# Low halves of expert 0 on GpSimd and a later start for expert 2's load, in a convolution and mixture-of-experts kernel

## The chip, the cores and the metric

One core of a Trainium2 chip runs the whole program. The metric is the device time of one execution in microseconds, the median of several runs. The engines are named as in the profile: PE (TensorE matrix products), PEld (its weight loads), DVE (VectorE), ACT (ScalarE), POOL (GpSimd), SP (SyncE, which here only issues DMAs). A q behind a name (SPq, ACTq) is that engine's sequencer.

## The reference

```python
# attention: softmaxed 7-tap causal filters, one for each of 8 heads of 24 channels
w = softmax(weight)                                  # 8 x 7
x_pad = concat([zeros(B, 6, 192), x], axis=1)        # x: 8 x 2880 x 192
attn[b, s, h, :] = sum_k w[h, k] * x_pad[b, s + k, h, :]
# mixture of experts over N = 23040 tokens of 192 values
g = argmax(attn @ w_group)          # 4 groups
e = argmax(attn @ w_expert[g])      # 4 experts in a group
y = relu(attn @ w1[g, e]) @ w2[g, e]     # 192 -> 1024 -> 192
out = softmax_g[g] * softmax_e[e] * y
```

All tensors are float32. Each token goes to one of 16 experts.

## The kernel before

**Units.** The tokens are cut into blocks of 120 (BT) and the blocks into units of 4, 8 or 12 (SIZES; unit 5 has 8 blocks, units 6, 7, 8, 9 and 10 have 12 each). `unit(u)` is a generator, and `step()` (L1147) moves the live units on by turns. A unit reads its input (`load_unit`, L254, DMAs at L250 and L252 on SP's queue; the tile xin has two buffers, and unit u asks for the input of unit u + 1 in its first step), convolves it with band matrices on PE (L506), copies the result from PSUM on ACT into xc or a spare tile and xcb (L511, L513), and stores both in DRAM in xcd (L515, L678, issued on ACT's queue). xc has two buffers (`room_tile`, L184), taken by every second unit, so that units 2, 4 and 6 follow each other there. Transposes (L527, L538) and small products (L600, L606) give the logits; DVE makes from them the choice and the weight of each token (L645 to L674, the last being the reciprocal that L678 stores with the rows) and its place in an expert's list (L685 to L736). POOL scatters the list into a table in DRAM with an indirect DMA (L738).

**Slots.** When five units are through, the list of the first portion is read back (L1209), and the main loop (L1402) begins: a slot is 256 tokens of one expert. Slot i gathers its rows by an indirect DMA from POOL (`gather`, L818, L829), transposes them on PE (`turn`, L848 and L850) and runs `hidden` (L872) and `back` (L892) in four steps f2 each. In the first portion there is one slot for each of experts 0 to 7, then more portions follow, and the units not yet routed are worked between the slots' steps. `finish` (L948) weighs the result and scatters it to the output (L965).

**High and low halves.** Products keep float32 precision by splitting each operand into a rounded high half and the rest, the low half. For an expert's weights, `weights()` (L757) takes four raw tiles out of a pool of six buffers, loads w1 into the first two (128 and 64 rows of 1024 values) and w2 into the last two (L765, L766, L771, all through `load`, L749, on SP's queue), and leaves four `split(k)` to be done: ah and al (k = 0), bb (k = 1) and the two halves of cw (k = 2, 3). Each has a copy on ACT (L786, L790, L798) and then a subtraction (L787, L791, L799), whose engine is `eng.get(k, nc.vector)`: DVE unless the dictionary `eng` names another. The first half of `hidden` likewise is an ACT rectifier (L886) and a DVE operation for its low half hl (L887); the list `lows` holds the latter in order.

**What sets the order.** Expert 0's weights are asked for in step 60 of the routing and split in steps 100 to 130, expert 1's are asked for in step 140 (KPRE, L1304 to L1314) and split in the 96 further steps before the main loop (L1319 to L1324). `{k: nc.gpsimd for k in PREG[e]}` (L1311) is their `eng`. Expert 0's raw tiles take buffers 2 to 5 of the pool, expert 1's 0 to 3 and expert 2's 4, 5, 0 and 1. Expert 2's weights are asked for in `open_slot(2)`, called in the first step of slot 0 (L1448), by L1296:

```python
weights(..., held=pi == 0 and e > 1, after=(gathers[0] if e == 2 else lows[2] if e == 3 else None) if pi == 0 else None)
```

`after` puts a wait on the loads for the named instruction: `gathers[0]` is the last gather of slot 0, `lows[0]` the first low half hl of slot 0. `held` keeps the loads of w2 back until the last step of slot i (L1456), where those of expert 2 wait for `lows[0]` too. The program's text gives each instruction a place, but the order on each engine's queue is chosen by the compiler's planner, which takes what is ready first by its own costs; `pin`, `issue_after` and `keep_in_program_order` are the exceptions written into the code. An engine works its queue in that order.

Of the kernel before, what the change touches and what calls it, by code (L numbers as in the profile page):

```python
# [35 lines left out]
def conv_moe_kernel(  # L36
# [20 lines left out]
    def pin(on, ins):  # L57

        return tc.keep_in_program_order(ins) if on and pinned[0] else ins

    B, S, D = x.shape
# [4 lines left out]
    F = w1.shape[3]  # L66
# [42 lines left out]
    PENG = lambda pi, e: None  # L109
# [16 lines left out]
    GL = 6  # L126
    GB = 4
    MARGIN = 5
    PREG = ((), ())
    RB = False  # L130
    PRE2 = 0
    NSK = 2
# [612 lines left out]
    lows = []  # L745

    gathers = []

    def load(dst, src, after=None):  # L749
        ins = nc.sync.dma_start(out=dst, in_=src)  # L750
        if after is not None:
            tc.add_manual_dep(
                ins.ins, after.ins.name,
                mybir.DependencyInfo(mybir.DependencyClass.Sync, mybir.DependencyReason.DATA), reason="later load")
        return ins

    def weights(r1, r2, eng=None, held=False, after=None):  # L757
        eng = eng or {}
        raw = [wraw.tile([P, F], F32, name="raw") for _ in range(4)]
        ra, rb = raw[0], raw[1]  # L760
        HF = NF // 2
        rc = [r[:, 0:HF * D].rearrange("p (f d) -> p f d", d=D) for r in raw[2:]]
        npin[0] += 1
        hold = tc.keep_in_program_order if NPIN[0] < npin[0] <= NPIN[1] else lambda ins: ins
        hold(load(ra, w1f[bass.ds(r1, P), :], after))  # L765
        hold(load(rb[0:D2], w1f[bass.ds(r1 + P, D2), :], after))  # L766

        def fetch(after=after):
            for k in range(2):
                loads.append(load(  # L770
                    rc[k], w2f[bass.ds(r2 + k * HF * P, HF * P), :].rearrange("(f p) d -> p f d", p=P), after))  # L771

        W = {}
        if held:
            W["fetch"] = fetch
        else:
            fetch()

        def split(k):
            if k == 0:  # L780
                W["ah"] = ah = wsp.tile([P, F], F32R, name="ah")
                W["al"] = al = wsp.tile([P, F], F32R, name="al")
                if 8 in eng:
                    nc.gpsimd.tensor_copy(out=ah, in_=ra)
                else:
                    pin(PINA, nc.scalar.activation(out=ah, in_=ra, func=AF.Copy))  # L786
                eng.get(k, nc.vector).tensor_tensor(out=al, in0=ra, in1=ah.bitcast(F32), op=ALU.subtract)  # L787
            elif k == 1:
                W["bb"] = bb = wsp.tile([P, F], F32R, name="bb")
                pin(PINB, nc.scalar.activation(out=bb[0:D2], in_=rb[0:D2], func=AF.Copy))  # L790
                eng.get(k, nc.vector).tensor_tensor(  # L791
                    out=bb[D2:P], in0=rb[0:D2], in1=bb[0:D2].bitcast(F32), op=ALU.subtract)
            else:
                if k == 2:
                    W["cw"] = wsp.tile([P, NF, 2, D], F32R, name="cw")
                cw = W["cw"]
                fs = slice((k - 2) * HF, (k - 1) * HF)
                pin(PINW, nc.scalar.activation(out=cw[:, fs, 0, :], in_=rc[k - 2], func=AF.Copy))  # L798
                eng.get(k, nc.vector).tensor_tensor(  # L799
                    out=cw[:, fs, 1, :], in0=rc[k - 2], in1=cw[:, fs, 0, :].bitcast(F32), op=ALU.subtract,  # L800
                )

        W["todo"] = [lambda k=k: split(k) for k in range(4)]
        return W
# [331 lines left out]
    def stages_to(n):  # L1136
        extra = sum(max(0, stages(n) - i * (SKEW2 + (SKEWX if n >= THIN else 0))) for i in range(1, LIVE2)) if n < NU else 0
        return sum(stages(u) for u in range(n)) + extra
# [8 lines left out]
    def step():  # L1147

        if routed[0] < NU and len(live) < lead[1] and (not live or max(live, key=lambda a: a[0])[1] >= (lead[0] and lead[0] + (SKEWX if routed[0] > THIN else 0) or SK[min(routed[0], len(SK)) - 1])):
            u = routed[0]  # L1150
            live.append([u, 0, unit(u, xin0 if u == 0 else None)])
            routed[0] += 1
        if not live:
            return
        done[0] += 1
        cur = live.pop(0)
        cur[1] += 1
        try:
            next(cur[2])
            live.append(cur)  # L1160
        except StopIteration:
            pass
# [68 lines left out]
    def tail_regs(get, n):  # L1231
        return [
            nc.values_load(
                get(c), engines=[ET.SP], min_val=0, max_val=mv, skip_runtime_bounds_check_because=OOB_WHY,
            )
            for c, mv in ((0, (E - 1) * D), (1, (E - 1) * F), (2, DUMMY))[:n]
        ]
# [28 lines left out]
    opened, gathered, turned = {}, {}, {}  # L1266
# [7 lines left out]
    def open_slot(i):  # L1274
        if i >= len(plan):
            return
        pi, e, s = plan[i]
        if closing:
            wait[0] -= 1
            if wait[0] <= 0 or closing[0] == pi:  # L1280
                open_portion(closing.pop())
        while (len(portions) - 1 if pi == "tail" else pi) not in idps:
            step()
            if closing:
                open_portion(closing.pop())
        rate[0] = max(
            [(stages_to(portions[q][0]) - done[0]) / (max(starts[q] - MARGIN - i, 1) * 2 * NF)
             for q in starts if q not in idps] + [0.0])
        while pi == "tail" and e not in ready:
            next(late[0])  # L1290
        if pi == "tail":
            W = weights(*tail_regs(lambda c: tab[0][0:1, e, c:c + 1], 2)) if s == 0 else opened[i - 1][0]
            ids = [idps["tail"][0:n, e, k:k + 1] for k, n in tail_cols(PIECES[e], s)]
            known = N
        else:
            W = pre.pop(e if pi == 0 else None, None) or weights(e * D, e * F, PENG(pi, e), held=pi == 0 and e > 1, after=(gathers[0] if e == 2 else lows[2] if e == 3 else None) if pi == 0 else None) if s == 0 else opened[i - 1][0]  # L1296
            ids = [idps[pi][:, e - portions[pi][1], k:k + 1] for k in (2 * s, 2 * s + 1)]
            known = sum(n for _, n in units[:portions[pi][0]]) * BT
        opened[i] = (W, ids)
        gathered[i] = gather(ids, known, width(i), i >= E)  # L1300

    pre = {}
    k = 0
    while routed[1] < portions[0][0]:  # L1304
# [3 lines left out]
        for i in [i for i, kk in enumerate(KPRE) if kk == k]:  # L1308
            e, q = divmod(i, 5)
            if q == 0 and e < 2:  # L1310
                pre[e] = weights(e * D, e * F, {k: nc.gpsimd for k in PREG[e]}, held=e > 0)  # L1311
            elif e < 2 and 4 * e + q <= KN:
# [20 lines left out]
    held = None  # L1333
# [68 lines left out]
    for i, (pi, e, s) in enumerate(plan):  # L1402
# [3 lines left out]
        W, ids = opened[i]  # L1406
        w = width(i)
        if i == len(plan) - 1:
            while W["todo"]:
                split_one(W)  # L1410
            held = []
# [80 lines left out]
```

## Time and profile before

| what | value |
|---|---|
| median of 3 runs | 1067.4 us (1065.37 to 1073.29) |
| the profiled execution | 1075.81 us, of which the span from first to last instruction is 1074.1 |
| busy in the span | PE 97%, DVE 69%, ACT 62%, POOL 48% |
| granted TensorE clock | 0.999 of full speed |

Busy times are the time in which an engine had an instruction under way; the ends of PE's instructions are modelled. In the timelines a row has the start, the time from there to the end of the last instruction merged into it, the engine, the line, the operation, the tile written and those read, their sizes and the count; brackets hold the engine's idle time just before and what ended it. A wait for several things is put down to the one that came last by the profile. The DMA share is the mean busy share of the core's 16 DMA engines.

### The profile page before, as it was taken

The page shows a single profiled execution, that of the slowest core. Times are in us where ns is not written, and L with a number is a line of the kernel's source. Part 1 is how long each engine was busy: PE and PEld are TensorE (multiplying, and loading weights), DVE is VectorE, ACT ScalarE, POOL GpSimd, SP SyncE. Part 2 cuts the span into 40 slices and gives each one's busy share as a digit, 9 for nine tenths or more (in the row PEclk, how much of TensorE's full clock was granted, in tenths as well). Part 3 has the DMA queues.
Part 4 walks back from the last instruction along what each step waited for, and adds up shares of the span by engine and source line. Part 5 has one row for each costly group of instructions (what it writes and reads, how often), then busy time and mean ns, then how long its engine had stood idle before and what let it go on. Part 6 is the DMA issues. An engine that isn't in the chain of part 4 may idle for free. (4 is left out here: it accounts for less than half of the span.)

```text
span 1074.1 us, 22328 instructions
## 1 busy us (share of the span) xinstructions
PE 1040.1 (97%) x7908; PEld 1013.9 (94%) x7908; DVE 745.0 (69%) x1790; ACT 661.7 (62%) x1486; POOL 520.2 (48%) x485
## 2 busy tenths in 40 slices
PE   6989999999999999999999999999999999999997
PEld 6878999999999999999999999999999999999997
DVE  4768888979888878867876666656566656556553
ACT  4556577755666656566666666656565666556653
POOL 2114334336546445565556655555565555455432
PEclk9999999999999999999999999999999999999999
DMA  8998897779889578345536432323233332323210
GB/s 200 259 227 215 205 225 203 180 213 235 204 211 203 127 191 187 106 116 106 156 76 176 114 99 75 115 68 110 67 100 104 95 100 71 92 78 98 65 32 26
DMA packets 192755, 148.53 MB, mean 138 GB/s; under 512 B 84616, under 2 KB 178099, under 8 KB 192638
## 3 DMA queue, kind: packets, MB, share of 16 engines
q1 hardware_dynamic: 126608, 92.89, 34.2%
q0 software_dynamic: 19392, 36.09, 12.5%
q10 hardware_dynamic: 46638, 18.07, 7.7%
q8 instruction: 63, 1.03, 0.4%
q14 instruction: 54, 0.44, 0.1%
HBM read 100.47 MB, written 36.46 MB: 127 GB/s over the span
## 5 line engine op out<-in xcount | busy, mean ns | idle before, releaser
L899 PE MATMUL po<-cw,hh 128*128 128x384 f32 x944 | 294.2, 369 | 0.4 <-ACT ys L957 0.4
L881 PE MATMUL ph<-xa,ah 128*128 128x256 f32 x944 | 258.8, 295 | 3.3 <-DVE hl L887 2.1
L886 ACT ACTIVATE hh<-ph 128x512 fp32r<-128x512 f32 x236 | 140.2, 596 | 174.3 <-PE ph L881 133.5
L903 PE MATMUL po<-cw,hl 128*128 128x192 f32 x944 | 236.4, 250 | 0.7 <-issue 0.7
L887 DVE SCALAR_TENSOR_TENSOR hl<-ph,hh 128x512 fp32r<-128x512 f32 x236 | 161.0, 687 | 104.5 <-ACT hh L886 79.0
L829 POOL DMA_INDIRECT xg<-xcd,idpt x137 | 145.1, 1059 | 179.3 <-ACT ys L957 74.8
L829 POOL DMA_INDIRECT xg<-xcd,idp x116 | 132.7, 1144 | 183.7 <-ACT ys L957 97.7
L881 PE MATMUL ph<-xb,bb 128*128 128x256 f32 x944 | 189.6, 282 | 0.5 <-issue 0.4
L881 PEld LDWEIGHTS ph<-xa,ah 128*128 128x128 f32 x944 | 178.4, 189 | 7.1 <-DVE hl L887 2.7
L903 PEld LDWEIGHTS po<-cw,hl 128*128 128x128 f32 x944 | 180.1, 191 | 1.7 <-issue 0.2
L899 PEld LDWEIGHTS po<-cw,hh 128*128 128x128 f32 x944 | 177.6, 188 | 2.3 <-ACT ys L957 0.6
L881 PEld LDWEIGHTS ph<-xb,bb 128*128 128x128 f32 x944 | 146.1, 190 | 1.0 <-issue 0.9
L965 POOL DMA_INDIRECT out<-ys,idpt x99 | 109.8, 1109 | 56.3 <-DVE ys L964 31.6
L881 PE MATMUL ph<-xa,al 128*128 128x256 f32 x472 | 133.9, 284 | 0.5 <-issue 0.5
L965 POOL DMA_INDIRECT out<-ys,idp x88 | 106.3, 1208 | 39.9 <-issue 16.2
L919 PE MATMUL ph<-xa,ah 128*128 128x384 f32 (+1 forms) x368 | 122.2, 335 | 2.9 <-DVE xc L925 1.5
L957 ACT ACTIVATE ys<-po,xg 128x384 f32<-128x384 f32 x164 | 92.0, 581 | 33.2 <-PE po L943 13.5
L864 ACT ACTIVATE xb<-pm 64x128 fp32r<-64x128 f32 (+2 forms) x342 | 94.9, 277 | 6.1 <-DVE xc L674 3.0
L881 PEld LDWEIGHTS ph<-xa,al 128*128 128x128 f32 x472 | 89.3, 189 | 1.7
L919 PE MATMUL ph<-xb,bb 128*128 128x384 f32 (+1 forms) x368 | 90.2, 326 | 0.0
L964 DVE TENSOR_TENSOR ys<-ys 128x192 f32<-128x192 f32 x179 | 61.3, 356 | 28.6 <-ACT ys L957 24.7
L799 DVE TENSOR_TENSOR cw<-raw,cw 128x768 fp32r<-128x768 f32 x80 | 76.1, 953 | 6.4 <-ACT cw L798 5.1
(264 smaller groups left out, 2115.6 us busy)
## 6 DMA issues: line engine op xcount, KB each, us to landing
raw<-in_moe_w SPq DMA_DIRECT2D x80, 384.0 KB
raw<-in_moe_w SPq DMA_DIRECT2D x40, 512.0 KB
raw<-in_moe_w SPq DMA_DIRECT2D x40, 256.0 KB
xcd<-xc ACTq DMA_DIRECT2D x11, 742.5 KB
xin<-in_x SPq DMA_DIRECT2D x7, 1134.0 KB
xin<-in_x SPq DMA_DIRECT2D x6, 1039.5 KB
xcd<-xcb ACTq DMA_DIRECT2D x13, 360.0 KB
xg<-xcd,idpt POOLq DMA_INDIRECT x137
```

The costliest lines, as they stand in the source:

```text
L799: eng.get(k, nc.vector).tensor_tensor(out=cw[:, fs, 1, :], in0=rc[k - 2], in1=cw[:, fs, 0, :].bitcast(F32), op=ALU.subtract,)
L829: ins = nc.gpsimd.indirect_dma_start(out=rows[0:n, to:to + size], out_offset=None, in_=xcd[0:known, :], in_offset=bass.IndirectOffsetOnAxi ...
L864: nc.scalar.activation(out=xb[h:h + D2, 0, c:c + k], in_=pb, func=AF.Copy)
L881: nc.tensor.matmul(out=hp[:, j], lhsT=wgt[:, fs], rhs=xx, start=i == 0, stop=i == len(ops) - 1)
L886: nc.scalar.activation(out=hh, in_=hp, func=AF.Relu)
L887: lows.append(nc.vector.scalar_tensor_tensor(out=hl, in0=hp, scalar=0.0, in1=hh.bitcast(F32), op0=ALU.max, op1=ALU.subtract,))
L899: nc.tensor.matmul(out=oo[t][:, 0:2 * D], lhsT=hh[:, j, ts], rhs=cw[:, f].rearrange("p a d -> p (a d)"), start=f == 0, stop=False,)
L903: nc.tensor.matmul(out=oo[t][:, 0:D], lhsT=hl[:, j, ts], rhs=cw[:, f, 0, :], start=False, stop=f == NF - 1,)
L919: nc.tensor.matmul(out=hp[:, 0:w], lhsT=wgt[:, fs], rhs=xx, start=i == 0, stop=i == len(ops) - 1)
L957: nc.scalar.activation(out=y, in_=oo[t][0:n, 0:2 * D], func=AF.Copy, scale=g)
L964: nc.vector.tensor_tensor(out=y[:, 0:D], in0=y[:, 0:D], in1=y[:, D:2 * D], op=ALU.add)
L965: nc.gpsimd.indirect_dma_start(out=outviews[nscat[0] % len(outviews)], out_offset=bass.IndirectOffsetOnAxis(ap=ids[t].bitcast(U32), axis=0 ...
```

## The change

Two settings are changed. PREG names, for expert 0, all four splits, so that its four subtractions (L787, L791 and L799 twice) are issued on POOL; the copies stay on ACT. And the loads of expert 2's w1 wait for `lows[0]` in place of `gathers[0]`.

```diff
@@ -126,7 +126,7 @@
     GL = 6
     GB = 4
     MARGIN = 5
-    PREG = ((), ())
+    PREG = ((0,1,2,3), ())
     RB = False
     PRE2 = 0
     NSK = 2
@@ -1293,7 +1293,7 @@
             ids = [idps["tail"][0:n, e, k:k + 1] for k, n in tail_cols(PIECES[e], s)]
             known = N
         else:
-            W = pre.pop(e if pi == 0 else None, None) or weights(e * D, e * F, PENG(pi, e), held=pi == 0 and e > 1, after=(gathers[0] if e == 2 else lows[2] if e == 3 else None) if pi == 0 else None) if s == 0 else opened[i - 1][0]
+            W = pre.pop(e if pi == 0 else None, None) or weights(e * D, e * F, PENG(pi, e), held=pi == 0 and e > 1, after=(lows[0] if e == 2 else lows[2] if e == 3 else None) if pi == 0 else None) if s == 0 else opened[i - 1][0]
             ids = [idps[pi][:, e - portions[pi][1], k:k + 1] for k in (2 * s, 2 * s + 1)]
             known = sum(n for _, n in units[:portions[pi][0]]) * BT
         opened[i] = (W, ids)
```

## Rows read from the trace of the kernel before

**Rows 1.** The page, busy us, share of the span, instructions.

```profile
PE 1040.1 (97%) x7908; PEld 1013.9 (94%) x7908; DVE 745.0 (69%) x1790; ACT 661.7 (62%) x1486; POOL 520.2 (48%) x485
```

**Rows 2.** Stages: busy us of each engine, granted clock, DMA share, GB/s.

```profile
40.00:60.00 20.00, 16.03 (x139) 13.89 (x139) 19.24 (x72) 11.53 (x35) 2.65 (x2) 1.00 1.08 266
...
80.00:84.00 4.00, 4.00 (x36) 3.67 (x35) 3.85 (x13) 3.86 (x12) 1.39 (x2) 1.00 0.38 28
84.00:88.00 4.00, 4.00 (x46) 3.99 (x46) 3.73 (x12) 2.83 (x8) 3.29 (x3) 1.00 0.65 137
...
100.00:120.00 20.00, 19.66 (x178) 18.79 (x177) 19.68 (x62) 11.94 (x25) 5.99 (x6) 1.00 1.09 275
```

**Rows 3.** Timeline of PE, 40 to 130 us.

```profile
49.19 0.59 PE L506 MATMUL pm<-xin,band 126*120 126x192 f32 x2 [1.00 <-DVE eold L723]
...
53.15 0.47 PE L732 MATMUL po<-ohv,ohl 120*128 120x32 f16 x12 [1.11 <-DVE ohv L713]
...
58.23 0.63 PE L527 MATMUL pm<-ident,spare 120*128 120x120 f32 x4 [1.61 <-ACT ta L530]
...
87.41 0.31 PE L848 MATMUL pm<-ident,xg 128*128 128x128 f32 x1
...
125.86 0.67 PE L506 MATMUL pm<-xin,band 126*120 126x288 f32 x2
```

**Rows 4.** Timeline of DVE, 40 to 115 us.

```profile
43.10 1.22 DVE L787 TENSOR_TENSOR al<-raw,ah 128x1024 fp32r<-128x1024 f32 x1
...
45.16 1.22 DVE L791 TENSOR_TENSOR bb<-raw,bb 64x1024 fp32r<-64x1024 f32 x1
...
47.12 0.44 DVE L674 RECIPROCAL xc<-se 120x48 f32<-120x48 f32 x1
...
53.00 0.95 DVE L799 TENSOR_TENSOR cw<-raw,cw 128x768 fp32r<-128x768 f32 x1
...
54.89 0.13 DVE L736 SCALAR_TENSOR_TENSOR lsi<-po,none 128x32 int32<-128x32 f32 x1
...
97.19 0.69 DVE L887 SCALAR_TENSOR_TENSOR hl<-ph,hh 128x512 fp32r<-128x512 f32 x1 [0.42 <-ACT hh L886]
...
110.54 1.22 DVE L787 TENSOR_TENSOR al<-raw,ah 128x1024 fp32r<-128x1024 f32 x1
```

**Rows 5.** Timeline of ACT and its queue, 45 to 125 us.

```profile
47.59 0.32 ACTq L678 DMA_DIRECT2D xcd<-xc  x1
...
57.30 0.41 ACT L511 ACTIVATE xc<-ph 120x288 f32<-120x288 f32 x1 [6.16 <-DVE ohx L657]
...
121.02 1.06 ACT L786 ACTIVATE ah<-raw 128x1024 fp32r<-128x1024 f32 x1 [4.78 <-PE pm L606]
```

**Rows 6.** Timeline of POOL, 0 to 85 us.

```profile
1.40 0.28 POOL masks.py:199 TENSOR_SCALAR_AFFINE_SELECT ident<-ident 128x128 f32<-128x128 f32 x1
...
3.57 2.17 POOL L456 MEMSET xg<- 128x588 f32 x4
...
43.47 1.69 POOL L738 DMA_INDIRECT idtab<-lsi,rowi  x1 [9.09 <-DVE lsi L736]
55.30 0.97 POOL L738 DMA_INDIRECT idtab<-lsi,rowi  x1 [10.14 <-DVE dd L646]
...
71.74 0.96 POOL L738 DMA_INDIRECT idtab<-lsi,rowi  x1 [8.16 <-DMA idtab<-lsi,rowi]
...
82.62 1.17 POOL L829 DMA_INDIRECT xg<-xcd,idp  x1 [2.41 <-DMA idp<-idtab]
```

**Rows 7.** Timeline of SP's queue, 84 to 112 us.

```profile
87.55 0.36 SPq L750 DMA_DIRECT2D raw<-in_moe_w  x1
...
88.47 0.45 SPq L252 DMA_DIRECT2D xin<-in_x  x1
...
104.43 7.77 SPq L750 DMA_DIRECT2D raw<-in_moe_w  x3
```

**Rows 8.** Waits of SP's queue, 20 to 140 us: total, times, longest.

```profile
SPq L750 <- DMA xg<-xcd,idp: 16.3, 1, 16.3
```

## The prediction

> **What bounds the kernel now.** I read the page's busy shares first: TensorE (PE) is busy 1040.1 us of 1074.1 [rows 1], so all its idle time together is 34.0 us and no edit of the preparation of weights can win more than the part of it that it touches. The table by stages comes next, because the edits act in the first 125 us. From 40 to 60 us PE is busy 16.03 of 20, VectorE (DVE) 19.24, GpSimd (POOL) 2.65, and the DMA engines are full (share 1.08); from 80 to 88 us their share is 0.38 and then 0.65, and from 100 to 120 it is 1.09 again [rows 2]. Third, PE's timeline with what ended each idle time: 1.00 us at 49.19 and 1.11 us at 53.15 ended by DVE, 1.61 us at 58.23 by ScalarE (ACT) [rows 3]. These are most of the 3.97 us that PE loses there, and I take the rest of the program as paid by PE's own work. So the question is whether DVE's share of these waits shrinks, and whether the loads that the second edit moves make a new one.
>
> **Part one, the low halves of expert 0 on POOL.** DVE loses four subtractions: 1.22 us (al, at 43.10), 1.22 us (bb, at 45.16) and two of 0.95 us (cw, the last at 53.00) [rows 4], in all 4.34 us out of a stretch in which it is 96% busy. POOL gets them: 1024 + 1024 + 768 + 768 = 3584 elements a partition. No row shows a two-input operation of POOL. The memset of xg writes 588 elements four times in 2.17 us, 0.92 ns an element, and gives 3.3 us; the affine select, with one input, takes 0.28 us for 128, 2.2 ns an element, and gives 7.8 us; twice that, if two inputs cost two passes, gives 15.8 us [rows 6]. I take 7.8, since the affine select is the nearest row (it reads and writes), and keep 3.3 and 15.8. What hides it is POOL's idle time: its scatter of unit 1 ends at 43.47 + 1.69 = 45.16 and the one of unit 2 starts after 10.14 idle us at 55.30 [rows 6]. All four behind the first scatter end at 45.2 + 7.8 = 53.0; at 15.8 they end at 61.0 and the scatter of unit 2 is 5.7 us late.
>
> Two chains run through the freed DVE time. The first: the reciprocal at 47.12 gates the store of unit 2's rows, issued at 47.59 on ACT's queue [rows 4, 5]. ACT then idles 6.16 us until 57.30, where it writes an xc tile [rows 5]; the row names a DVE operation, but the pool has two buffers of this tile and the one wanted is the one that the store reads, so I read the wait as the store's landing. PE's 1.61 us end with it. Two of the subtractions (2.44 us) stand ahead of the reciprocal. The second chain: the list of unit 2 at 54.89 gates its scatter at 55.30; each later scatter waits for the landing of the one before (8.16 us before 71.74), then come the list's reload, the gather at 82.62, and the transposes at 87.41, which PE reaches without idling [rows 3, 4, 6]. Both chains thus meet at 87.41, and a gain must come from both. The second has all four subtractions ahead of it, but POOL itself is free only at 53.0, so it moves by 55.3 - 53.0 = 2.3 us. I take the smaller, **-2.3 us**. It is nothing if the landings, in full DMA queues, do not move; -4.3 if all of DVE's saving arrives; and +5.7 us at the dear end of POOL's price.
>
> Other waits on these four: expert 1's w2 goes into the buffers of expert 0's w1 and waits on SP for al and bb, behind it the input of unit 7. With POOL's two at 2.2 us each (1024 elements) behind the first scatter, bb ends at 49.6 instead of 46.4; but that input waits anyway for the convolution at 49.19, which ends at 49.78 [rows 3]. Nothing. The halves' own readers are the first slot's matmuls, past 87.41. Nothing.
>
> **Part two, expert 2's w1 held.** Its two loads (128 and 64 rows of 4 KB: 512 and 256 KB) wait at the head of SP's queue for 16.3 us for the first gather and go at 87.55 [rows 7, 8]. They will wait for the first low half, 97.19 + 0.69 = 97.88 [rows 4], 10.3 us later. The first subtraction that reads them runs on DVE at 110.54 [rows 4]; 768 KB at the 275 GB/s of 100 to 120 us [rows 2] take 2.9 us, so they have some 12 us for 3 and their own use costs nothing. What stands behind the waiting load matters more. Its other instructions behind it are the rest of expert 2's loads, with the same wait, expert 3's with a later one, and inputs of units. On record the input of unit 10 (126 rows by 11 blocks of 768 bytes, 1039.5 KB, beside its small first block) goes behind it, at 88.47 [rows 7]. In the program this load is older, and its buffer is free before the first low half exists, so I expect the planner to put it ahead: out at about 82 us, where the DMA engines idle 0.62 and 0.35 of two 4 us stretches [rows 2], 3.9 us of work; the load needs 3.9 us at 275 GB/s. Its reader runs at 125.86 [rows 3], so it wins nothing by itself, but it now runs beside the first gather (82.62 to 87.41). Bounds: 0, if it fills idle time alone, and 3.9 us, if it goes wholly first. As nearly all of it fits the hole I take a quarter, **+1.0 us**.
>
> Then the backlog. Between 88 and 98 us the engines lose 1.04 MB to the hole before and 0.77 MB to later; the stretch from 98 us on, full until past 120, has 0.77 MB more to move, 2.8 us at 275 GB/s. What comes last in it is expert 3's w1, issued from 104.43 and awaited by ACT until 121.02 (4.78 us, put down to a PE operation long over) [rows 5, 7]. From 100 to 120 us PE idles only 0.34 us [rows 2]: logits and the second layer of an older step cover the wait. A longer wait has less cover. Bounds 0 and 2.8; I take **+0.8**, a third, for a cover that has held 4.78 us at almost no loss.
>
> Sum: -2.3 + 1.0 + 0.8 = -0.5 us. The profiled execution took 1075.81 us (span 1074.1 and 1.7 around it), so it would take 1075.3. It lies 8.4 us above the median of the runs, 1067.4, which I carry over: **1066.9 us**.
>
> **The rivals.** (a) POOL's reads block DVE. Place: DVE's two-input work from 45 to 53 us; price: POOL's 7.8 us stand in for DVE's 4.34, +3.5 us instead of -2.3 on both chains, and with 1.0 and 0.8 a total of +5.3, 1072.7 us. It decides once DVE waits for more than 4.34 of POOL's 7.8 us. For it: most of DVE's rows in that stretch are two-input ones on a full engine. Against it: POOL's rows of before read too little to show it either way; the scatter at 43.47 took 1.69 us against 0.97 at 55.30 [rows 6], while DVE's al kept its 1.22. The Trainium skill, in "SBUF — State Buffer", section "Who interferes with whom", says that a DVE instruction with two SBUF inputs contends with a GpSimd instruction that reads SBUF, and that the second to issue blocks until the first is through. No row of this trace shows such a pair; by that rule this rival is the outcome.
> (b) The hold doesn't free the queue: the planner leaves unit 10's input behind the held load. Then 1.04 + 0.77 MB go after 98 us, 6.6 us at 275 GB/s, before expert 3's; less a cover of 2 us, +4.6, with -2.3 a total of +2.3, 1069.7 us. For it: this order on record [rows 7]. Against it: the load is older and ready first.
> (c) The wins arrive whole: both chains move 4.3 us, no collision, 1063.1 us. For it: POOL at the memset's rate ends by 48.5. Against it: scatters and stores that land in full queues.
>
> **How the numbers follow.** The forecast 0.4, (a) 0.25, (b) 0.1, (c) 0.25. From (c), with 2 us for the spread of the runs below their median (1065.37 to 1073.29), the range begins at 1061; above (a) stands the mix of a dear POOL with the backlog, +5.7 + 1.0 + 0.8, 1074.9, of which I take in 1074. A measurement of this kernel tells about 1% (10.7 us) from no change, and none of the cases reaches it. So faster by over 1% gets 0.04, slower 0.04 and within 1% 0.92; the two ends are for an order of instructions that the planner changes elsewhere.
>
> **What would show it.** Right: four POOL subtractions of about 2.2 and 1.7 us between 41 and 54 us; DVE busy clearly less in 40 to 60; the scatter of unit 2 near 53 instead of 55.30; ACT's write of xc near 55; unit 10's input before 84 us and expert 2's w1 at about 96 to 98; the transposes of the first slot at 86; ACT's wait for expert 3 ending past 121. Wrong: DVE rows longer, or idle behind POOL, while a POOL subtraction runs (a); unit 10's input after 97 us (b); PE idle for several us at the first transposes, or in a stretch past 140 us, which I have priced at nothing.

## The result, and the profile after

The changed kernel takes 1077.28 us (median of 6 runs, 1074.93 to 1081.76) where the kernel before takes 1066.84 beside it (6 runs, 1064.93 to 1073.29): a ratio of 1.0103, 95% interval 1.0071 to 1.0134, 10.4 us slower. The forecast was 1066.9, with a range that ended at 1074. The profiled execution of after took 1076.8 us, span 1075.1.

The table by stages of the changed kernel (busy us of PE, PEld, DVE, ACT, POOL, with the count of instructions in brackets, then the granted clock, the DMA engines' share, GB/s) is to be set beside [rows 2]:

```profile
40.00:60.00 20.00, 16.17 (x110) 14.45 (x110) 18.43 (x48) 9.36 (x27) 10.33 (x6) 0.77 0.97 228
60.00:80.00 20.00, 17.52 (x127) 14.11 (x125) 12.23 (x56) 12.32 (x33) 3.47 (x4) 0.97 0.73 169
80.00:100.00 20.00, 18.25 (x145) 17.13 (x143) 11.78 (x37) 11.19 (x28) 10.75 (x10) 0.88 0.94 228
100.00:120.00 20.00, 19.23 (x122) 17.27 (x122) 14.64 (x55) 10.09 (x23) 0.98 (x1) 0.78 0.58 160
```

Busy times hardly tell that anything is wrong: PE is as busy as before from 40 to 60 us (16.17 against 16.03) and DVE less (18.43 against 19.24). What tells it is the count of instructions beside them (PE x110 against x139, DVE x48 against x72) and the granted clock, 0.77, 0.97, 0.88 and 0.78 where the kernel before had 1.00. Less work is done in the same busy time.

First DVE. POOL's four subtractions in the changed kernel's timeline of POOL, and its scatters of units 1 and 2, to be set beside [rows 6]:

```profile
41.19 2.40 POOL L787 TENSOR_TENSOR al<-raw,ah 128x1024 fp32r<-128x1024 f32 x1 [7.18 <-ACT ah L786]
45.35 0.99 POOL L738 DMA_INDIRECT idtab<-lsi,rowi  x1 [1.76 <-DMA xcd<-xcb]
46.41 2.35 POOL L791 TENSOR_TENSOR bb<-raw,bb 64x1024 fp32r<-64x1024 f32 x1
49.82 3.72 POOL L799 TENSOR_TENSOR cw<-raw,cw 128x768 fp32r<-128x768 f32 x2 [1.06 <-DMA raw<-in_moe_w]
58.77 0.98 POOL L738 DMA_INDIRECT idtab<-lsi,rowi  x1 [5.23 <-DVE dd L646]
```

and DVE's timeline of the same kernel, beside [rows 4]:

```profile
41.29 2.57 DVE L653 TENSOR_TENSOR oh<-sc,mx 120x240 f32<-120x240 f32 x1
...
46.66 2.28 DVE L653 TENSOR_TENSOR oh<-sc,mx 120x160 f32<-120x160 f32 x1
...
49.05 0.45 DVE L674 RECIPROCAL xc<-se 120x48 f32<-120x48 f32 x1
...
50.43 1.42 DVE L691 TENSOR_TENSOR pos<-cum,off 120x192 f32<-120x192 bf16 x1
...
51.77 1.81 DVE L724 TENSOR_TENSOR rows<-eold,sel 128x17 f32<-128x17 f32 x1
...
58.31 0.18 DVE L736 SCALAR_TENSOR_TENSOR lsi<-po,none 128x32 int32<-128x32 f32 x1
```

Four of these instructions (L653 twice, L691, L724) in a second profile of the kernel before (a run named e5, below):

```profile
42.28 0.40 DVE L653 TENSOR_TENSOR oh<-sc,mx 120x240 f32<-120x240 f32 x1
...
48.48 0.33 DVE L653 TENSOR_TENSOR oh<-sc,mx 120x160 f32<-120x160 f32 x1
...
49.79 0.36 DVE L691 TENSOR_TENSOR pos<-cum,off 120x192 f32<-120x192 bf16 x1
50.07 0.17 DVE L724 TENSOR_TENSOR rows<-eold,sel 128x17 f32<-128x17 f32 x1
```

Read the ends: POOL's al runs from 41.19 to 43.59, and DVE's two-input operation that begins at 41.29 ends at 43.86; POOL's bb ends at 48.76 and DVE's at 48.94. DVE counts as busy while it stands. Over the four, against e5, it loses 2.17 + 1.95 + 1.06 + 1.64 = 6.8 us and was relieved of 4.34. So the reciprocal of unit 2 comes at 49.05 (47.12 in [rows 4]) and its scatter at 58.77 (55.30 in [rows 6]): later, not sooner.

Second, SP's queue in the changed kernel, beside [rows 7], and PE's wait for the first gather, where [rows 3] has none:

```profile
86.38 0.39 SPq L252 DMA_DIRECT2D xin<-in_x  x1
108.16 2.29 SPq L750 DMA_DIRECT2D raw<-in_moe_w  x4
```

```profile
94.00 0.33 PE L848 MATMUL pm<-ident,xg 128*128 128x128 f32 x1 [1.75 <-DMA xg<-xcd,idp]
```

Unit 10's input now goes out in front of expert 2's w1 and beside the first gather, as forecast, but PE can begin the transposes of the gathered rows only at 94.00, 7 us after the gather's second piece was issued (86.95), and waits 1.75 us for it.

Third, the clock. Two-us windows of the changed kernel, same columns as the stages:

```profile
48.00:50.00 2.00, 0.79 (x5) 0.40 (x4) 1.47 (x3) 1.37 (x4) 0.94 (x2) 1.00 0.54 93
50.00:52.00 2.00, 1.65 (x10) 1.53 (x9) 1.78 (x4) 2.00 (x6) 1.90 (x2) 0.71 0.82 183
52.00:54.00 2.00, 2.00 (x12) 2.00 (x11) 2.00 (x4) 0.86 (x5) 1.54 (x1) 0.50 1.09 286
...
92.00:94.00 2.00, 0.26 (x2) 0.00 (x0) 1.97 (x6) 0.53 (x2) 1.68 (x2) 1.00 1.13 238
94.00:96.00 2.00, 2.00 (x13) 1.88 (x14) 1.45 (x7) 0.46 (x2) 1.70 (x2) 0.81 1.04 192
96.00:98.00 2.00, 2.00 (x12) 2.00 (x11) 0.00 (x0) 1.38 (x4) 1.39 (x3) 0.50 0.75 203
...
108.00:110.00 2.00, 2.00 (x13) 1.69 (x12) 0.96 (x6) 1.12 (x3) 0.00 (x0) 0.78 0.36 78
```

PE is busy 0.79 of the two us from 48, and from about 51 to 61 us its granted clock is 0.50, the lower of its two levels (1.2 GHz); it is busy 0.26 us of the two from 92, and from about 95 to 108.5 the clock is 0.50 again. What that means for the work is seen in one matmul line on either side, from PE's timeline of the same kernel:

```profile
90.51 0.55 PE L606 MATMUL ph<-wr,ta 128*120 128x40 f32 x4
...
100.36 0.94 PE L606 MATMUL pm<-wr,ta 128*120 128x40 f32 x4
```

Where the time is lost can be read from one line of ACT's timeline, the cast of each expert's w1 (line 786). The table has it for expert 0 and expert 3, the time between them, and the time that PE spends at 1.2 GHz from 40 to 120 us, worked out from the four stages as the sum of 2 x (1 - granted clock) x 20:

| profile | expert 0 | expert 3 | between | PE at 1.2 GHz |
|---|---|---|---|---|
| before, of [rows 1 to 8] | 40.31 | 121.02 | 80.71 | 0 |
| before, second profile (e5) | 41.03 | 120.92 | 79.89 | 0 |
| before, third profile (e17) | 41.23 | 129.27 | 88.04 | 24 |
| after | 40.02 | 129.86 | 89.84 | 24 |
| after, second profile (e6) | 41.64 | 135.35 | 93.71 | 28 |
| after, third profile (e16) | 38.60 | 131.84 | 93.24 | 28 |
| part one alone (e14) | 39.19 | 122.30 | 83.11 | 7 |
| part two alone (e15) | 38.17 | 124.64 | 86.47 | 14 |

From expert 3's cast to the last cast all eight take 887.5 to 888.9 us, except the first profile of before, which took 895.35. The whole difference thus lies between 40 and 130 us; and the first profile of before had lost some 8 us further on that the median does not have (3.7 us of it stand in two waits put down to "remote", a name that comes up again below), so the two profiled times (1075.81 and 1076.8) are alike though the medians aren't.

### The profile page after: what moved, and what is told of

The parts are those of the page before. It is cut to its first block, busy times and chain, and to the rows that moved or that the text cites. A ratio compares the mean times of both kernels' runs of the same rounds, so it can differ in the third digit from the quotient of the medians.

```text
span 1075.1 us, 22334 instructions
## 1 busy us (share of the span) xinstructions
PE 1047.0 (97%) x7908; PEld 1022.2 (95%) x7908; DVE 749.9 (70%) x1786; ACT 665.4 (62%) x1486; POOL 531.2 (49%) x489
## 5 line engine op out<-in xcount | busy, mean ns | idle before, releaser
L829 POOL DMA_INDIRECT xg<-xcd,idp x116 | 135.1, 1164 | 183.0 <-ACT ys L957 96.9
L922 ACT ACTIVATE spare<-ph 128x384 fp32r<-128x384 f32 (+1 forms) x92 | 43.4, 472 | 61.6 <-PE ph L919 61.6
```

The costliest lines, as they stand in the source:

```text
L829: ins = nc.gpsimd.indirect_dma_start(out=rows[0:n, to:to + size], out_offset=None, in_=xcd[0:known, :], in_offset=bass.IndirectOffsetOnAxi ...
L922: nc.scalar.activation(out=H2[:, j, 0:w], in_=hp[:, 0:w], func=AF.Relu)
```

## The experiments

They went to several chips. On some the kernel before takes about 1066 us, on others 1083 to 1091; each is compared with the kernel before on its own chip. None changes what is computed; where work is added, its results go nowhere.

### What GpSimd's reading does to VectorE

e5 is the kernel before and e6 the changed kernel, on one chip with e7 and e8. In those two DVE keeps its subtractions, and POOL does four operations of 588 elements behind each of expert 0's four casts, into a gather buffer that is filled later. The order on every engine is the same in both; only what POOL does differs:

```
-PREG = ((), ())
+PREG = ((0,1,2,3), ())     (now: where POOL works beside)
+4 times behind each cast:
+    e7: nc.gpsimd.memset(scratch[:, 0:588], 0.0)
+    e8: nc.gpsimd.tensor_copy(out=scratch[:, 0:588], in_=src[:, 0:588])
```

> The kernel before once more, for its trace on the chip of these runs. Theory A: no stretch of the lower clock before 60 us (PE idles there in four pieces of about 1 us and 1.6 us, as in the first trace). If the second lower stretch, at the first slot, shows here too, then it isn't the change that brings it.

> The whole change once more, beside the kernel before on one chip. Theory A: the loss of part one, +4 to +6 us, on every chip, and up to +5 us more where the first gather's lateness brings the lower clock, so +4 to +11. Rival (the loss is peculiar to the first chip): within 1.5 us.

> DVE keeps its four subtractions; POOL only writes beside them (four memsets of 588 columns behind each of the four ACT copies, some 9 us in all; they write zeros over the fourth gather buffer, which holds zeros). Theory A (it is POOL's reading of SBUF that holds DVE): DVE's two-input rows as long as before (0.41 for the compare of 240 elements, 1.22 for al) and within 1.5 us of before. Rival E (any operation of POOL holds DVE): DVE rows of 0.4 us stretched to the end of a POOL row, +4 us or more.

> The same program with copies in place of the memsets: POOL reads 588 columns of the raw tile and writes them over the fourth gather buffer, in the same order on every engine. Theory A: DVE's two-input rows that start while a copy runs end with it, DVE is later by up to the copies' 9 us before 60 us, PE idles and its clock falls: +4 to +9 us over the memset kernel. Rival F (DVE is held by something else, such as POOL's semaphores or the order of its instructions): the same time as with memsets.

Against a median of 1066.21 us of before (21 runs, 1063.52 to 1073.24): e6 1080.01, ratio 1.0111 (1.0081 to 1.0141), by the medians 13.8 us slower where 11 was expected at most; e7, POOL writing alone, 1068.17, 1.0012 (0.999 to 1.0034), not to be told from before; e8, POOL reading as well, 1072.53, 1.0058 (1.0034 to 1.0082). DVE's timeline in e7:

```profile
39.81 0.40 DVE L653 TENSOR_TENSOR oh<-sc,mx 120x240 f32<-120x240 f32 x1
...
46.26 0.95 DVE L799 TENSOR_TENSOR cw<-raw,cw 128x768 fp32r<-128x768 f32 x1
...
50.26 0.95 DVE L717 TENSOR_TENSOR ohl<-iop,posh 120x1536 bf16<-120x1536 f16 x1
```

and in e8:

```profile
41.65 0.88 DVE L653 TENSOR_TENSOR oh<-sc,mx 120x240 f32<-120x240 f32 x1
...
49.16 1.43 DVE L799 TENSOR_TENSOR cw<-raw,cw 128x768 fp32r<-128x768 f32 x1
...
55.84 1.42 DVE L717 TENSOR_TENSOR ohl<-iop,posh 120x1536 bf16<-120x1536 f16 x1
```

e7's rows are those of the kernel before; e8's are each about half a us longer, roughly what is left of one short POOL copy (0.73 us in its first row). So the reading holds DVE, not POOL's being busy nor its writing, and a kernel in which DVE's work is unchanged gets slower by it: 6.3 us above the kernel before, 4.4 above e7. The Trainium skill, "SBUF — State Buffer", section "Who interferes with whom", says just that: a DVE instruction with two SBUF inputs contends with a GpSimd one that reads SBUF, not with one that only writes. The runs agree, with 0.40 us against 2.57 in the change itself.

### The two parts alone, and the whole, on one chip

The first part is the one line of PREG, the second the one line of the load's wait; e17 is the kernel before.

```
e14: -PREG = ((), ())                       e15: -after=(gathers[0] if e == 2 ...
     +PREG = ((0,1,2,3), ())                     +after=(lows[0] if e == 2 ...
e16: both
```

> Only the four subtractions go to GpSimd. Theory (VectorE held by GpSimd's reads, and a stretch of about 10 us at a granted clock of 0.50 after TensorE's waits at 45 to 51 us, costing half of its length): 4 to 7 us above the kernel before of this call. Rival (this part makes the whole difference): as far above it as the changed kernel in this call, within 2 us.

> Only expert 2's load is held behind the first low half. Theory: unit 10's input goes out beside the first gather, TensorE waits 1 us or more for it and a low stretch of 10 us or more follows: 3 to 7 us above the kernel before of this call, and with the first part's difference about the changed kernel's. Rival (the part is free alone): within 2 us of the kernel before, and the changed kernel's difference is more than the sum of its parts.

> The changed kernel beside its two parts on the same chip. Theory (the losses of the two parts come at different places and add): its difference from the kernel before is the sum of those of the two parts, within 3 us. Rival (the parts overlap, or one brings the other's loss about): it is below the larger of the two plus 2 us, or above the sum by over 3 us.

> The kernel before, looked at on this call's chip. Theory: on a chip where its median is near 1067 us its granted clock stays at 1.00 from 40 to 130 us, as in its two profiles so far; where its median is near 1090 us it loses time itself to low stretches there, so that less is left for the change to lose. Rival: no low stretch on any chip.

Against 1066.24 us (14 runs, 1064.41 to 1068.85): part one 1070.85, ratio 1.0043 (1.003 to 1.0055), +4.6 us; part two 1073.32, 1.0075 (1.0047 to 1.0103), +7.1; both 1078.52, 1.0096 (1.0066 to 1.0127), +12.3. The sum of the parts is 11.7: they add. The rivals of e14, e15 and e16 fall (the four runs of e16 and the five of e15 leave some 3 us of doubt in each).

In e14 the list of unit 2 is late, as in the changed kernel: its scatter starts 18.44 us after expert 0's cast (57.63 - 39.19), in e5 14.97 (56.00 - 41.03), so 3.5 us later. PE's timeline and the first stage of e14:

```profile
50.48 0.59 PE L506 MATMUL pm<-xin,band 126*120 126x192 f32 x2 [2.77 <-DVE eold L723]
```

```profile
40.00:60.00 20.00, 15.71 (x109) 13.83 (x109) 18.52 (x49) 9.36 (x28) 10.35 (x6) 0.83 0.80 196
```

PE waits 2.77 us for a row that DVE could not get to ([rows 3] has 1.00 for this line), and the clock falls behind it.

In e15 DVE is untouched. SP's queue, PE's timeline and the stage of the first gather, in e15:

```profile
79.88 0.39 SPq L252 DMA_DIRECT2D xin<-in_x  x1
103.94 4.77 SPq L750 DMA_DIRECT2D raw<-in_moe_w  x4
```

```profile
87.86 0.30 PE L848 MATMUL pm<-ident,xg 128*128 128x128 f32 x1 [2.37 <-DMA xg<-xcd,idp]
...
88.92 0.47 PE L848 MATMUL pm<-ident,xg 128*128 128x128 f32 x1 [0.66 <-DMA xg<-xcd,idp]
```

```profile
80.00:100.00 20.00, 16.52 (x109) 15.56 (x109) 10.09 (x36) 6.56 (x16) 10.65 (x9) 0.71 0.62 157
```

The gather, issued at 80.35 and 81.75, is waited for until 87.86 and 88.92: 3.0 us of PE, and the clock is low for 14 us from 88. (The weight load ahead of the first of these transposes has "issue" as its releaser, so that the gather ends this wait is the profile's inference; e4 below bears it out.) The DMA engines' busy tenths from 80 to 92 us, in 40 slices, in e15:

```profile
DMA  0369447999999999999999999973046200939788
```

and in the kernel before, whose gather was issued at 82.62:

```profile
DMA  5337934100005778999666510093976958997767
```

In e15 every slice from 82.1 to 87.8 us is full while the gather runs; before, three slices are between the gather's issue and the transposes at 87.41. The held load itself costs nothing that shows: expert 2's w1 goes out at 103.94 and is cast at 109.65 with no idle time of ACT before it, and PE idles 0.3 us from 100 to 120.

e17 is the surprise: this one run of the kernel before took 1076.3 us. Its stages from 40 to 100 us:

```profile
40.00:60.00 20.00, 18.67 (x126) 16.69 (x125) 16.96 (x60) 11.04 (x31) 2.65 (x2) 0.76 1.06 254
60.00:80.00 20.00, 16.18 (x109) 12.85 (x107) 12.05 (x55) 10.97 (x29) 3.57 (x4) 0.93 0.73 175
80.00:100.00 20.00, 20.00 (x129) 18.25 (x130) 9.15 (x29) 10.37 (x25) 8.55 (x8) 0.71 0.76 202
```

The instructions are the same. There are two stretches at 1.2 GHz, 24 us in all, and it takes 88.04 us from expert 0's cast to expert 3's instead of 80.3 (the mean of its two other profiles): 7.7 us, or 0.32 us for each us at the lower clock. That is the price of the clock by itself, with no edit in it; it comes from one run, so it is a rough one. By it the 9.5 us that after lost between the two casts are 7.7 of clock and 1.8 of the waits themselves, e16's 12.9 are 9 and 4, e15's 6.2 are 4.4 and 1.8.

The mean granted clock of each run without a profile is on record too, and gives a second price from many runs. On this chip and that of e5 the kernel before has 0.996 to 0.999 in 33 of 35 runs, none of them above 1069.87 us; the other two, at 0.991 and 0.992, took 1073.24 and 1072.66. The 16 runs of the changed kernel, on three chips, have 0.986 to 0.995. As 2 x (1 - clock) x span that is some 4 us at 1.2 GHz before and 23 after, on average. Four runs of the changed kernel with 0.992 to 0.995 (some 14 us at 1.2 GHz) took 1075.6 us on average, the other twelve (26 us) 1079.6: 0.34 us for each us. Brought down to the 4 us of the kernel before, the changed kernel would take some 1072 us, 5 above the 1066.9 that the kernel before takes on average. So of 11.7 us between the two averages some 6.6 go with the clock and some 5 with the waits themselves: an estimate, by which the clock is a little over half of the loss, less than e17's price alone makes it. In e8 it is less: 7 us at 1.2 GHz from 40 to 120 against 4 in e7, for 4.4 us of time.

Of e17's expectation the first half failed (the kernel before can fall to the lower clock on a chip where its median is 1066); its rival, that it never does, failed too. Its second half, on the slower chips, is borne out by the clocks on record, below.

### The same on chips where the kernel before is slower

e1 and e9 are part one, e2 and e10 part two. e3 is part two with unit 10's input held behind the first gather as well, so that the gather runs alone; e11 is the changed kernel with that hold; e4 is the kernel before with unit 10's input put in front of expert 2's w1, both still behind the gather; e12 is the changed kernel with eight more transposes of the identity between the two pieces of the first slot's transposes, to fill PE's wait.

```
e3, e11 (the input of unit 10 waits for the first gather):
-hold=lambda ins: pin(0 < u <= PINL, ins)
+hold=lambda ins: wait_for(ins, gathers[0]) if u == 10 else pin(0 < u <= PINL, ins)
e4: +with tc.issue_after(<unit 10's input>): hold(load(ra, ...))    (expert 2 alone)
e12, in turn(), first slot, ahead of the second piece's transposes:
+[nc.tensor.transpose(px[:, P:2 * P], ident, ident) for _ in range(8)]
```

> Part one alone. Theory A (POOL's subtractions hold DVE's two-input operations, PE idles and its clock falls to half for some 10 us around 51 to 61 us; the rest of the loss belongs to part two): +4 to +6 us, near 1072; the first cast of expert 1 on ACT at about 76.7 as in the changed kernel (71.7 before), and no stretch at the lower clock past 65 us. Rival B (the whole loss comes from part one and is only carried on): +9 to +11 us. Rival D (part one is the gain and part two the whole loss): -2 to 0 us.

> Part two alone; only SP's order changes, unit 10's input in front of expert 2's first load. Theory A (that input runs beside the first gather, which lands about 4 us later, and PE idles before the first slot's transposes and falls to half clock): +3 to +8 us, the wait of the transposes put down to the gather. Rival B: within 1 us of before. Rival C (the loss is expert 2's own lateness and the backlog behind it): +3 to +5 us, but with the transposes at 87 to 88 us as before and the loss only past 103 us.

> Part two, with the input of unit 10 also waiting for the first slot's last gather, as it did by its place in the queue before. Theory A: the loss goes, within 1.5 us of before, the transposes back at 87 to 88 us at full clock, although expert 2's loads still start at about 98. Rival C: +3 to +5 us, as the loads of expert 2 are as late as in the whole change.

> The kernel before with one thing changed: the input of unit 10 goes in front of expert 2's first load, which still waits for the first gather only. Theory A: the same loss as part two alone, +3 to +8 us, with the gather landing late. Rival C: within 1 us of before, since expert 2's loads start as early as before.

> Only the four subtractions go to GpSimd; expert 2's load waits for the first gather as before. Theory (three causes: GpSimd's reads hold VectorE, the input beside the first gather makes it land late, and TensorE's waits are followed by stretches at its lower clock): VectorE's two-input rows beside the four GpSimd rows take 1.4 to 2.6 us again, the lists of the units come 3 to 4 us later, one stretch of about 10 us at a granted clock of 0.50 starts at about 51 us, none of 13 us at 95: about 1071 us, 4 to 6 us above before. Rival (the whole loss is this part's): 10 us or more above before, 1076 or more, with both low stretches.

> Only expert 2's load is held behind the first low half; VectorE keeps the subtractions. Theory: lists as early as before, unit 10's input issued beside the first gather, whose second piece lands 4 to 6 us after its issue; TensorE waits 0.5 to 2 us for it at the first transposes; 0 to 2 us above before where the clock stays, 4 to 7 us where a low stretch follows. Rival (the input is hidden here, as the forecast had it): no wait of TensorE over 0.5 us for the gather, within 1 us of before.

> The changed kernel with one wait more: unit 10's input waits for the first gather, so that the gather runs alone; every engine's order is the changed kernel's. Theory: the gather's second piece lands 2 to 4 us after its issue instead of 7, TensorE waits under 0.5 us for it, no stretch at 0.50 from 95 us on: 4 to 7 us below the changed kernel, about 1071. Rival (the gather is late from the list alone, the input costs nothing): within 2 us of the changed kernel, 1076 or more, the wait of 1.75 us stays.

> The changed kernel with 8 more transposes of the identity (128x128, about 0.11 us each, 0.9 us in all) between the first and the second piece's transposes of the first slot, into columns that the second piece's transposes then write. They fill half of the 1.75 us that TensorE waits there. Theory (the waiting is what the lower clock follows): the second low stretch goes or becomes much shorter, 4 to 6 us below the changed kernel, about 1072. Rival (the stretch comes from something else): granted clock 0.50 from about 95 to 108 us as in the changed kernel and its time, within 2 us.

| kernel | median, us | before, us | ratio, 95% interval |
|---|---|---|---|
| e1 part one | 1094.39 | 1090.71 | 1.0043 (1.0013 to 1.0074) |
| e2 part two | 1089.86 | 1090.71 | 1.0023 (0.9984 to 1.0062) |
| e3 part two, input later | 1089.56 | 1090.71 | 0.9994 (0.9951 to 1.0037) |
| e4 input first | 1092.68 | 1090.71 | 0.999 (0.9949 to 1.0032) |
| e9 part one | 1095.76 | 1089.88 | 1.0065 (1.0028 to 1.0102) |
| e10 part two | 1090.75 | 1089.88 | 1.0023 (0.9982 to 1.0063) |
| e11 both, input later | 1092.3 | 1089.88 | 1.0037 (1.0001 to 1.0073) |
| e12 both, wait filled | 1093.9 | 1089.88 | 1.0056 (1.0023 to 1.009) |

Part one is slower here too. Part two can't be told from no change in time, though e10's trace has the waits and the fall of the clock that e15's has (3.63 us at the first transposes, 0.50 from 93 to 106 us). In e2's trace neither is there: the input left at 84.65, 4 us behind the gather's second piece (80.62), PE reached both transposes without idling (at 92.31 and 92.56, late behind a 4.14 us wait of ACT of the kind told of next), and the clock is 1.00 from 80 to 120 us; that run, 1086.23 us, was the fastest of its ten.

Two things set these chips apart. The first is the clock: the kernel before has 0.987 to 1.000 in its 85 runs there, with medians of 0.993, 0.993 and 0.995 on the three chips, so it spends some 11 to 16 us at 1.2 GHz itself and has less to lose by the change. The second is waits whose releaser the profile calls "remote", a name for nothing in this core's program. Each of the ten profiles from these chips has 9 to 20 of them, spread over the whole program, 15 to 44 us in sum and mostly on ACT; the nine other profiles beside the first of before have none. Part one alone has them in the stages of the change (e9), and so has a kernel whose loads are all in the order of before (e13, below):

```profile
106.07 0.41 DVE L645 TENSOR_REDUCE mx<-pm 120x60 f32<-120x240 f32 x1 [6.13 <-remote]
```

```profile
90.54 0.57 ACT L530 ACTIVATE ta<-pm 128x480 f32<-128x480 f32 x1 [3.44 <-remote]
```

What they are was not found. They bury an effect of a few us, so the runs on these chips bear on the argument by what their rows show rather than by their times.

e12 tested nothing: in its profile PE waited 3.07 us ahead of the first piece, so the added transposes stood behind the wait; its low stretch there was about 3 us long, which one profile doesn't settle. e3 and e4 can't be told from no change either: in e3's trace PE stands 2.24 us soon after the transposes, put down to ACT's xa, which itself had waited 3.37 us for "remote", and the granted clock is 0.73 from 80 to 100 us; in e4's PE waits 2.19 and 0.53 us for the gather, with 0.71:

```profile
87.62 0.30 PE L848 MATMUL pm<-ident,xg 128*128 128x128 f32 x1 [2.19 <-DMA xg<-xcd,idp]
```

In e4 expert 2's w1 goes out as soon as the gather lets it, so the input in front of it is enough to make the gather late. In e11 the wait for the gather is gone (transposes at 91.09 and 91.56 with no idle time), but the loss is not; e18, below, has the same and shows why it tells little.

### The input behind the gather, and VectorE relieved without GpSimd

e18 is e3's kernel once more. e13 is the kernel before with expert 0's two w2 splits put later, where DVE has idle time, so that DVE is relieved of 1.9 us between 48 and 54 us and POOL reads nothing.

```
e13: -KN = 4                              +KN = 2
     -if k in KSPL:                       +if k in KSPL or k in (8, 14):
     -    split_one(opened[1][0])         +    split_one(opened[k not in (8, 14)][0])
```

> The second part alone (expert 2's load held behind the first low half), with unit 10's input held behind the first gather, so that the gather runs alone. Theory (the second part loses because the input beside the gather makes TensorE wait and a low stretch follows): on a chip where the kernel before takes about 1067 us, no wait of TensorE over 0.7 us at the first transposes, no stretch at 0.50 from 88 to 102 us, within 2 us of the kernel before, 5 us or more below the second part alone. Rival (the late load of expert 2 is what costs): 5 to 8 us above the kernel before, as the second part alone.

> The kernel before with expert 0's two w2 splits (casts and subtractions) taken out of the early loop and put behind the 8th and the 14th step of the loop that waits for the first lists, where VectorE has idle time; all stay on VectorE, GpSimd reads nothing. Theory (a relief of VectorE at 48 to 54 us is worth what the forecast gave it, when nothing reads beside it): the list of unit 2 comes 1 to 2 us sooner, 1 to 2 us below the kernel before. Rival (the relief is worth nothing, another engine sets the lists): within 0.5 us, or the splits are late for the first slot and it is 1 us or more above.

Again a chip on which the kernel before is slower, 1083.43 us (23 runs): e18 1085.84, ratio 1.0024 (0.9991 to 1.0058); e13 1085.58, 1.002 (0.9987 to 1.0053). Neither can be told from no change. The theory of e18 was for a chip on which the kernel before takes about 1067 us, and it did not get one. PE and DVE in e18 at the first transposes:

```profile
84.86 0.33 PE L848 MATMUL pm<-ident,xg 128*128 128x128 f32 x1
...
90.10 0.69 PE L600 MATMUL pm<-wr,ta 128*120 128x80 f32 x2 [3.67 <-ACT ta L540]
```

```profile
90.64 0.19 DVE L735 TENSOR_SCALAR none<-ph 128x32 f32<-128x32 f32 x1 [2.08 <-remote]
```

With the gather alone on the queues PE reaches both transposes without the wait (the gather, issued at 79.05 and 80.45, is there by 84.86). But PE stands 3.67 us soon after, put down to an ACT copy, while DVE waits 2.08 us and ACT 1.09 for "remote", and the low clock comes from 88 to 102 us all the same. e11 has the same stop, of 4.63 us. The input's transfer, issued at 85.27, runs meanwhile, but it need not be the cause: on these chips "remote" ends waits all over the program, near the first slot's transposes in e1, e9 and e13 too, where this input is not moved, and it ends none in e15, on a faster chip, where the input runs beside the gather. So e18 shows that the gather is in time when the input is held back, and not what that is worth: no run on a chip without these waits separates the late load of expert 2 from the early input. What speaks against the late load is that PE never waits for expert 2's weights in either e15 or e18.

In e13 DVE is busy 16.63 us from 40 to 60, 2.6 less than in [rows 2], but the scatter of unit 2 comes 11.51 us after the one of unit 1 (53.04 - 41.53) where [rows 6] has 11.83 (55.30 - 43.47), as have, within 0.01, e2, e3, e4, e5, e10, e15 and e18: 0.3 us for 1.9 us of DVE's work. The theory of that run, that the relief is worth 1 to 2 us when nothing reads beside it, fell. No version was found that beats the kernel before.

## Why the prediction was wrong, point by point

**The price of POOL's work** was right: 7.8 us forecast, 2.40 + 2.35 + 3.72 = 8.5 measured, 2.4 ns an element.

**"A gain must come from both chains ... I take the smaller, -2.3"** failed, on two counts. DVE does not run freely beside POOL: rival (a) is what happened, and its price was right where it was placed (+3.5 us on unit 2's list, 3.5 measured in e14). I had given it 0.25 since no row of the trace showed such a pair, and let the rule of the Trainium skill that I named there weigh little. The row that I put against it rather speaks for it: the scatter of unit 1 takes 1.68 to 1.71 us in each of the twelve profiles in which DVE's al runs beside it, and 0.99 in each of the eight in which al is POOL's and done before, which fits the two engines getting in each other's way already in the kernel before, there at POOL's cost. And the term itself was too large: by e13 two of the four subtractions off DVE bring the list 0.3 us, so the load of these two is not what sets it. The other two were not tried alone. Part one came to +4.6 instead of -2.3.

**The order on SP's queue** was right: the input went ahead of the held load, and rival (b) fell. It left at 86 us in the changed kernel and not at 82, since the lists were late; with DVE undisturbed (e15) it left at 79.88.

**"As nearly all of it fits the hole I take a quarter, +1.0"** is the term of part two that was mis-sized: the waits were 3.0 us in e15, three times the term and within its bounds of 0 and 3.9, and part two came to +7.1 with the clock behind them. The hole of [rows 2] was a mean over four us; the input's transfer and the gather wanted the same six (82.1 to 87.8 us, all full), and the gather is the small one that PE waits for.

**The backlog, +0.8**, did not show: ACT waited 2.30 us ahead of expert 3's cast in e15 and in the changed kernel, as in the other two profiles of the kernel before (2.38 in e5, 2.30 in e17) and less than the 4.78 of [rows 5], and expert 2's weights were in time.

**The clock** was in no term. I took each wait of PE at its own length. In each of the three profiles of the changed kernel single waits of 0.35 to 3.9 us were followed, in two places, by 10 to 17 us at 1.2 GHz, and by the estimate above some 6.6 of 11.7 us go with that. What is left at equal clock, some 5 us, is near rival (a)'s +5.3 (1072.7): it had the waits about right and left out what follows them. The upper end of the range (1074) had been added up from a dear POOL and a backlog that did not come, and left out the same. Rival (c) fell with the forecast.

**Carrying over the 8.4 us** between the profiled execution and the median was right: they were lost past 130 us, where both kernels do the same.

## What to carry to other kernels

Work given to GpSimd is not free because GpSimd idles: if it reads SBUF while VectorE runs operations with two SBUF inputs, VectorE stands for as long (here 2.57 us in place of 0.40), and its rows, not its idle time, show it. A large transfer that is moved up beside a small one that an engine waits for can make the small one late (here 3.0 us), though it fits the idle time of the queues on average. And a wait of TensorE is to be priced with the clock that may follow it: compare the granted clock and the count of instructions by stage, since the busy times can stay the same. Where each run's mean clock is on record, it prices the clock without a profile.

## What the runs showed of the hardware that was not expected

TensorE's fall to 1.2 GHz is not settled by the length of the wait. In e5 PE idled 2.73 us in one piece and the clock stayed at 1.00:

```profile
74.36 0.72 PE L506 MATMUL ph<-xin,band 126*120 126x288 f32 x2 [2.73 <-DMA xin<-in_x]
```

In e17, the same program, it was 0.78 and then 0.50 behind shorter waits:

```profile
49.67 0.19 PE L685 MATMUL pm<-cum,tri 120*128 120x16 bf16 x1 [0.36 <-ACT spare L511]
...
50.61 1.00 PE L506 MATMUL pm<-xin,band 126*120 126x192 f32 x2 [0.72 <-DVE eold L723]
```

```profile
50.00:51.00 1.00, 0.39 (x1) 0.39 (x2) 1.00 (x6) 1.00 (x4) 0.00 (x0) 0.78 1.14 171
51.00:52.00 1.00, 1.00 (x6) 1.00 (x5) 1.00 (x5) 1.00 (x6) 0.00 (x0) 0.50 1.25 176
```

So the kernel before can fall too, without any edit, but seldom: by the clocks on record clearly in two of 35 runs, beside e17. By the same clocks each of the 16 runs of the changed kernel spent some 11 to 30 us at 1.2 GHz. Of 41 runs of the kernel before on chips where its median is about 1066 none was above 1073.3, and of the 16 none was below 1074.5. What decides whether a wait is followed by a fall was not found. A clock that never fell was not tried in the changed kernel: the filled wait of e12 missed its place.
